# Gated linear attention and an ELU feed-forward in one kernel: blocks of 256 tokens taken in pairs from the fifth on

## The chip, the cores and the metric

The kernel runs on one core of a Trainium2 chip. The metric is the time of one execution on the device in microseconds (us), measured on runs without a profile; beside it there is one profiled execution with a trace of every engine. The engines are TensorE (PE, with its weight loads as PEld), VectorE (DVE), ScalarE (ACT), GpSimd (POOL) and SyncE (SP), which issues nearly all DMAs.

## The reference

```python
# q, k, v, alpha: (4, 8, 768, 48); w_in (384, 2048), w_out (2048, 384), all float32
for t in range(S):                       # per batch and head
    state = alpha[:, :, t, :, None] * state + einsum('bhd,bhe->bhde', k[:, :, t], v[:, :, t])
    y[:, :, t] = einsum('bhd,bhde->bhe', q[:, :, t], state)
x = y.transpose(0, 2, 1, 3).reshape(3072, 384)
h = x @ w_in
g = where(h > 0, h, exp(minimum(h, 0)) - 1)
out = g @ w_out
```

A recurrence over 768 tokens with a decay per token and channel, then two products with an ELU between them.

## The kernel before

The 3072 tokens are 24 windows of 128 (index i, six per batch) and 12 blocks of 256 (index b, two windows each). The state of a batch starts anew with every sixth window.

*Attention, per window.* L and LV load q, k, alpha and v. SC forms the running product P of the decays (a scan on VectorE), LN and EX its reciprocal R (ScalarE), KA, KB, KC and SQ scale k and q with them (POOL and DVE), T transposes k in 32x32 blocks on VectorE (eight instructions for a quarter g of the window's four). Then PE: U forms the two half-window updates of the state, S the scores of each half-window; both write a pair of PSUM banks named q. VectorE reads those banks: MK masks the scores (two parts), UA, UB and UC carry the state over the two halves and to the next window. Y multiplies state and masked scores into y, a bank of its own. XH (ScalarE) and XL (VectorE) split y into a high and a low part in f32r, written to the tile xt, which is the moving operand of the feed-forward; XD moves the channels of the last head pair to their rows by DMA.

*Feed-forward, per block b and j = 0 to 7.* A(b, j) multiplies 256 rows of w_in^T with x of the block: two slices f of 128 rows, each with 9 products (3 channel groups, and high x high, high x low, low x high), 256 columns each, into one bank h of 128 x 512. RA, RB (ScalarE), RC (VectorE) make the ELU, GH (ScalarE) and GL (VectorE, in some early blocks POOL) split it. O(b, j) multiplies with w_out into two banks per block, one for each 128 tokens: 12 products of 384 columns. Z copies the two banks out (ScalarE) and stores them. CA, CB, LC, V, VP check ranges of the weights, P and y for a slow path that is not taken here.

*Order.* Two tables written out by hand set the order: START names every step once with its indices up to O(3, 2), and STEADY is a table that function steady() unrolls for g = 4 to 13. One turn for one g is called a visit here: window indices stand relative to 2g, those of A to O relative to 8g (A.-3 is j = 5 of the block before, O.-5 is j = 3 of it), Z relative to g. Each engine executes its own steps nearly in the order of the tables; semaphores between engines and the reuse of buffers do the rest. All PSUM tiles share one pool of eight banks (psa, tag "pa"): a bank that q, y or h held goes to the next tile when its last reader is done. The x tile of a block is in a pool of two.

In STEADY of before a visit's Y is that of windows 2g and 2g + 1, and U and S are those of 2g + 2 and 2g + 3. The lines of the profile: U L368, S L323, Y L452 (L447 early), A L650, O L703, RA L658, RB L663, RC L669, GH L675, GL L689, MK L351, UA and UB L405 (UA on ScalarE L403 in windows 6, 12, 18), UC L434, SC L201, T L284, SQ L253, XH L506 and L507, XL L529 and L533, XD L540, Z L712, CA L601, CB L606. In the changed kernel most of them are three later up to L540, and nine or more later from A on.

Of the kernel before, what the change touches and what calls it, by code (L numbers as in the profile page):

```python
# [8 lines left out]
F32 = mybir.dt.float32  # L9
F32R = mybir.dt.float32r  # L10
# [70 lines left out]
MK.2.1 UC.2 XD.1 ZV.4 O.-4 XD.0 RC.-3 CB.-12 SC.4 RB.-2 A.-1 PC.3 GH.-3 RC.-2 A.0 LN.4 GL.-3 UA.3 EX.4 RA.-1
GH.-2 LC.-11 MK.3.0 L.6 MK.3.1 UB.3 CA.-11 A.1 RA.0 KA.4 L.5 RB.-1 GL.-2 RC.-1 A.2 RB.0 UC.3 CB.-11 RA.1 GH.-1
RC.0 O.-3 KB.4 RB.1 SC.5 KC.4 LC.-10 GL.-1 LN.5 GH.0 EX.5 RC.1 T.4.1 O.-2 A.3 VP.0 CA.-10 T.4.2 GL.0 GH.1 A.4
T.4.3 KA.5 O.0 RA.2 GL.1 RB.2 RA.3 CB.-10 LV.5 RC.2 PC.4 GH.2 KB.5 RB.3 GL.2 LC.-9 O.1 O.-1 KC.5 RA.4 O.2 SQ.4
T.5.2 CA.-9 RB.4 RC.3 CB.-9 RC.4 GH.3 T.5.1 GH.4 T.5.0 GL.3 T.4.0 T.5.3 LC.-8 SQ.5 Z.-1 GL.4
"""

@with_exitstack
def gla_elu_ffn(ctx: ExitStack, tc: tile.TileContext, qka, vv, vn, wgt, out):
    nc = tc.nc  # L90
# [348 lines left out]
    xt = {}  # L439
# [14 lines left out]
                         start=start, stop=True, skip_group_check=True)  # L454

    def xs(i):
        blk, half = divmod(i, 2)
        if blk not in xt:
            xt[blk] = xpool.tile([128, 2, NC, 2, W], F32R, name="xt", tag="xt")
        return xt[blk][:, half]  # L460


    @tok
    def YL(i):
        d = win[i]
        if i >= DIRECT:
            return
# [32 lines left out]
    @tok  # L500
    def XH(i):
        d = win[i]
        x, y = xs(i), d["y"]
        if i >= DIRECT:
            y3 = d["y3"] = work.tile([128, 2, W], F32R, name="y3", tag="y3")
            nc.scalar.activation(out=y3[:, 0], in_=y[:, 3], func=AF.Copy, accum_out=chk_y[:, 1, i:i + 1])  # L506
        nc.scalar.activation(out=x[:, :, 0], in_=y[:, 0:3], func=AF.Copy, accum_out=chk_y[:, 0, i:i + 1])  # L507

    def rest(out, upper):

        nc.tensor.matmul(out, lhsT=minus, rhs=upper, start=False, stop=True, skip_group_check=True)  # L511

    @tok
    def XP(i):
        d = win[i]
        rest(d["y"][:, 0:3], xs(i)[:, :, 0])
        if i >= DIRECT:
            rest(d["y"][:, 3], d["y3"][:, 0])

    @tok  # L520
    def XL(i):
        d = win[i]
        x, y = xs(i), d["y"]
        if i >= DIRECT:
            y3 = d["y3"]
            if i in XPE:
                nc.scalar.copy(out=y3[:, 1], in_=y[:, 3])
            else:
                nc.vector.tensor_tensor(out=y3[:, 1], in0=y[:, 3], in1=y3[:, 0].bitcast(F32), op=ALU.subtract)  # L529
        if i in XPE:  # L530
            nc.scalar.copy(out=x[:, :, 1], in_=y[:, 0:3])
        else:
            nc.vector.tensor_tensor(out=x[:, :, 1], in0=y[:, 0:3], in1=x[:, :, 0].bitcast(F32), op=ALU.subtract)  # L533
# [10 lines left out]
    wgts = [None] * (2 * NJ)  # L544
# [92 lines left out]
    ff, ops_ = {}, {}  # L637

    @tok
    def A(b, j):  # L640
        x = xt[b]
        h = psa.tile([128, 2, BLK], F32, name="h", tag="pa")
        ff[b, j] = dict(h=h)
        for f in range(2):
            k = 0
            t = wgts[2 * j]
            for c in range(NC):
                ws = slice(f * DM + c * 128, f * DM + c * 128 + 128)
                for wi, xi in ((0, 0), (0, 1), (1, 0)):
                    nc.tensor.matmul(h[:, f, :], lhsT=t[:, wi, ws], rhs=x[:, :, c, xi].rearrange("p a x -> p x a"),  # L650
                                     start=(f == 0 and k == 0), stop=(k == 8), skip_group_check=True)
                    k += 1

# [37 lines left out]
    @tok  # L691
    def O(b, j):
        d = ff.pop((b, j))
        gh, gl = d["gh"], d["gl"]
        if j == 0:
            ops_[b] = [psa.tile([128, 512], F32, name="o", tag="pa") for _ in range(2)]
        for m in range(2):
            o = ops_[b][m]
            ms = slice(m * 128, m * 128 + 128)
            for f in range(2):  # L700
                t = wgts[2 * j + 1]
                for k, (gt, wi) in enumerate(((gh, 0), (gh, 1), (gl, 0))):
                    nc.tensor.matmul(o[:, 0:DM], lhsT=gt[:, f, ms],  # L703
                                     rhs=t[:, wi, f * DM:f * DM + DM].rearrange("p (a x) -> p x a", a=2),
                                     start=(j == 0 and f == 0 and k == 0),
                                     stop=(j == NJ - 1 and f == 1 and k == 2))

    @tok
    def Z(b):
        for m in range(2):  # L710
            ot = gpool.tile([128, DM], F32, name="ot", tag="ot")
            nc.scalar.copy(out=ot, in_=ops_[b][m][:, 0:DM])  # L712

            q = nc.sync if b < NBLK - 1 else nc.scalar
            q.dma_start(out=out[b * BLK + m * 128:b * BLK + m * 128 + 128, :], in_=ot)
        del ops_[b], xt[b]
# [33 lines left out]
    start = [t.split(".") for t in START.split()]  # L750
# [220 lines left out]
```

## Time and profile before

| | us |
|---|---|
| median of 3 runs | 479.66 (479.53 to 479.87) |
| profiled execution | 478.73 |
| its span, first to last instruction | 476.8 |
| PE busy in it | 469.3 |
| VectorE busy | 380.0 |
| ScalarE busy | 299.2 |
| POOL busy | 124.0 |

Matmuls are pipelined, so the length of one (277 ns for one of 256 columns on the page) is not what it costs in a row of them; the chain of work that ended last, in order of time, gives start, length and count of each piece on the path, and a piece divided by its count gives that cost. An fp32 product of the attention stands there as two records. A row of a view by windows of time has each engine's busy time with its count of instructions, the granted clock, the DMA share and GB/s. Rows of groups and of the timeline name the line, engine, operation, tiles out<-in, shapes and count.

### The profile page before, as it was taken

The numbers are of one execution on the slowest core, as the hardware profiler recorded it, in microseconds if no ns is written. First come the engines' busy times: TensorE is split into PE (matmuls) and PEld (weight loads), VectorE is DVE, ScalarE is ACT, GpSimd is POOL, SyncE is SP. The second block draws the span as 40 slices with busy tenths as digits, with TensorE's granted clock in tenths as the row PEclk, the third lists the DMA queues.
The fourth block names the chain that finished last, engine by engine and source line by source line (L and its number), as shares of the span: only waits on it lengthen the run. The fifth ranks groups of instructions, "written<-read, shape, count | busy, mean of one in ns | idle before, by whom it ended". The sixth has DMA issues, their size and how long they took to land.

```text
span 476.8 us, 13298 instructions
## 1 busy us (share of the span) xinstructions
PE 469.3 (98%) x5438; PEld 450.3 (94%) x5438; DVE 380.0 (80%) x770; ACT 299.2 (63%) x696; POOL 124.0 (26%) x111
## 2 busy tenths in 40 slices
PE   8999999999999999999999999999999999999995
PEld 4889999999999999999999999999999999999995
DVE  6989999789889979869989989878988998344321
ACT  4586668764764668756766765757765666554432
POOL 3012332534564602502602602602602500000000
PEclk9999999999999999999999999999999999999999
DMA  8999330712326056235235335334333321210011
GB/s 307 414 414 409 118 84 16 229 55 78 110 101 200 1 151 204 69 112 206 61 115 180 90 113 176 95 114 172 101 104 113 100 69 52 66 43 10 2 36 38
DMA packets 20483, 61.14 MB, mean 128 GB/s; under 512 B 2880, under 2 KB 7872, under 8 KB 20416
## 3 DMA queue, kind: packets, MB, share of 16 engines
q1 hardware_dynamic: 20128, 59.83, 37.3%
q8 instruction: 45, 0.74, 0.7%
q10 hardware_dynamic: 288, 0.39, 0.2%
q14 instruction: 22, 0.18, 0.1%
HBM read 53.53 MB, written 4.72 MB: 122 GB/s over the span
## 4 chain that ended last, share of the span: by engine, by line
PE 98%; ACT 0%; DVE 0%; POOL 0%; issue 0%; POOLq 0%; DVEq 0%
PE h L650 42%; PE o L703 39%; PE y L452 4%; PE q L368 2%; PE y L447 2%; PE q L323 2%; PE wp L126 2%; PE sc L339 1%; PE wd L623 1%; PE tp L274 1%; PE y L492 1%; PE u L386 1%; PE yl L447 0%; PE wd L511 0%; POOL gl L689 0%
## 5 line engine op out<-in xcount | busy, mean ns | idle before, releaser
L650 PE MATMUL h<-xt,w 128*128 128x256 f32 x1728 | 204.8, 277 | 0.5 <-DVE r L669 0.2
L650 PEld LDWEIGHTS h<-xt,w 128*128 128x128 f32 x1728 | 198.5, 192 | 4.2 <-issue 1.6
L703 PE MATMUL o<-w,gh 128*128 128x384 f32 x768 | 188.2, 327 | 0.0
L703 PEld LDWEIGHTS o<-w,gh 128*128 128x128 f32 x768 | 132.8, 189 | 0.5
L703 PE MATMUL o<-w,gl 128*128 128x384 f32 x384 | 125.6, 327 | 0.0
L658 ACT ACTIVATE r<-h 128x512 f32<-128x512 f32 x96 | 56.8, 594 | 41.7 <-PE h L650 34.5
L675 ACT CAST gh<-h 128x512 fp32r<-128x512 f32 x79 | 45.9, 583 | 58.4 <-DVE h L669 35.3
L284 DVE STREAM_TRANSPOSE kn<-qka 32x128 f32<-32x128 f32 x256 | 77.4, 302 | 4.0
L689 DVE TENSOR_TENSOR gl<-h,gh 128x512 fp32r<-128x512 f32 x79 | 54.1, 688 | 28.4 <-ACT gh L675 27.3
L703 PEld LDWEIGHTS o<-w,gl 128*128 128x128 f32 x384 | 72.6, 189 | 0.6
L223 POOL TENSOR_TENSOR qka<-qka,R 128x512 f32<-128x512 f32 x18 | 23.1, 1283 | 155.9 <-DVE gl L689 109.4
L669 DVE SCALAR_TENSOR_TENSOR h<-r,h 128x512 f32<-128x512 f32 x79 | 53.0, 688 | 12.1 <-ACT r L663 11.4
L663 ACT ACTIVATE r<-r 128x512 f32<-128x512 f32 x96 | 59.5, 634 | 0.9
L351 DVE TENSOR_TENSOR st<-q,mask 64x256 f32<-64x256 f32 x72 | 30.4, 422 | 9.0 <-ACT vs L403 7.2
L253 POOL TENSOR_TENSOR st<-qka,P 64x512 f32<-64x512 f32 x30 | 36.0, 1199 | 1.6
L228 POOL TENSOR_TENSOR R<-P,R 128x512 f32<-128x512 f32 x20 | 24.4, 1221 | 33.9 <-DVE qka L223 32.5
L689 POOL TENSOR_TENSOR gl<-r,gh 128x512 fp32r<-128x512 f32 x17 | 24.1, 1425 | 25.4 <-ACT gh L675 16.9
L201 DVE TENSOR_TENSOR_SCAN P<-qka,first 128x516 f32<-128x516 f32 x24 | 29.5, 1229 | 1.3 <-DMA qka<-in_qka_dram 0.8
L210 ACT ACTIVATE R<-P 128x512 f32<-128x512 f32 x24 | 15.1, 631 | 17.8 <-DVE P L201 17.8
L601 ACT ACTIVATE ck<-ck 128x384 f32<-128x384 f32 x32 | 22.2, 694 | 5.6 <-DMA ck<-in_wgt_dram 5.6
L606 ACT ACTIVATE ck<-ck,lim 128x384 f32<-128x384 f32 x32 | 24.6, 768 | 0.1
L233 DVE SCALAR_TENSOR_TENSOR qka<-R,qka 128x512 f32<-128x512 f32 x24 | 19.9, 827 | 1.5 <-POOL R L228 1.3
(105 smaller groups left out, 448.4 us busy)
## 6 DMA issues: line engine op xcount, KB each, us to landing
qka<-in_qka_dram SPq DMA_DIRECT2D x22, 770.0 KB, 5.6
raw<-in_wgt_dram SPq DMA_DIRECT2D x16, 768.0 KB, 13.4
ck<-in_wgt_dram SPq DMA_DIRECT2D x32, 384.0 KB, 3.3
vs<-in_vv_dram SPq DMA_DIRECT2D x36, 192.0 KB, 3.3
out_dram<-ot SPq DMA_DIRECT2D x22, 192.0 KB, 2.0
vs<-in_vv_dram SPq DMA_DIRECT2D x6, 384.0 KB, 9.9
xt<-y SPq DMA_DIRECT2D x40, 48.0 KB, 2.2
qka<-in_qka_dram SPq DMA_DIRECT2D x2, 512.0 KB, 4.8
```

Source lines behind the costliest of these rows:

```text
L201: nc.vector.tensor_tensor_scan(out=P.rearrange("p n w -> p (n w)"), data0=t[:, 2 * NP * W:], data1=first.rearrange("p n w -> p (n w)"), in ...
L253: eng(SQV, i).tensor_tensor(out=st[r, a], in0=d["q"][r], in1=pw(i)[r], op=ALU.mult)
L284: nc.vector.transpose(out=kn[32 * t:32 * t + 32, :, 32 * g:32 * g + 32], in_=d["kt"][32 * g:32 * g + 32, :, 32 * t:32 * t + 32])
L351: nc.vector.tensor_tensor(out=d["st"][r, a, :, c * C:(c + 1) * C], in0=d["s4"][a][o], in1=mask[o].unsqueeze(1).broadcast_to([64, NP, C]), ...
L606: nc.scalar.activation(out=t, in_=t, func=AF.Relu, scale=-1.0, bias=lim, accum_out=chk_w[:, 1, f:f + 1])
L650: nc.tensor.matmul(h[:, f, :], lhsT=t[:, wi, ws], rhs=x[:, :, c, xi].rearrange("p a x -> p x a"), start=(f == 0 and k == 0), stop=(k == 8) ...
L658: nc.scalar.activation(out=r, in_=d["h"], func=AF.Relu, scale=-1.0)
L663: nc.scalar.activation(out=d["r"], in_=d["r"], func=AF.Exp, scale=-1.0)
L669: nc.vector.scalar_tensor_tensor(out=d["g"], in0=d["r"], scalar=-1.0, in1=d["h"], op0=ALU.add, op1=ALU.max)
L675: nc.scalar.copy(out=gh, in_=d["g"])
L689: q.tensor_tensor(out=gl, in0=d["g"], in1=d["gh"].bitcast(F32), op=ALU.subtract)
L703: nc.tensor.matmul(o[:, 0:DM], lhsT=gt[:, f, ms], rhs=t[:, wi, f * DM:f * DM + DM].rearrange("p (a x) -> p x a", a=2), start=(j == 0 and f ...
```

## The change

From block 4 on (PB = 4), blocks 2n and 2n + 1 are a pair. One x tile holds the four windows of a pair. A(b, j) then takes one slice of 128 rows of w_in^T (row r = 8 (b mod 2) + j of 16) and the 512 tokens of the pair: 9 products of 512 columns into the bank h, where there were 18 of 256. O(b, j) takes that slice into four banks that stay open over both blocks of the pair: 3 products in each of four banks, where there were 6 in each of two. Z works once per pair: four copies, two on ScalarE and two on VectorE, from four buffers. In STEADY the visit that has U and S of a window now has its Y too (Y.2 and Y.3), so y of a window comes a visit earlier, and Y of windows 8 and 9 stands at the end of START. The scratch for dynamic DMAs shrinks to 2048 bytes. Blocks 0 to 3 are computed as before.

```diff
+PB = 4
 ...
 GL.3.3 O.3.0 TB.11 CB.3 SQ.10 PC.10 O.3.1 TA.11 LC.4 O.3.2
+Y.8 XH.8 XL.8 XD.8 Y.9 XH.9 XL.9 XD.9
 ...
 STEADY = """
-A.-3 Y.1 XH.1 Y.0 XH.0 A.-2 XL.1 RA.-3 O.-5 RA.-2 XL.0 LV.4 U.2 CA.-12 V.0 RB.-3 S.2 UA.2 MK.2.0 U.3 UB.2 S.3
...
+U.2 S.2 L.5 A.-3 MK.2.0 UA.2 UB.2 MK.2.1 UC.2 V.0 PC.3 SC.4 CA.-12 CB.-12 O.-5 U.3 S.3 RA.-3 LN.4 L.6 LC.-11 UA.3
+Y.2 MK.3.1 EX.4 MK.3.0 XH.2 O.-4 RB.-3 Y.3 XH.3 XL.2 A.-2 RC.-3 UB.3 GH.-3 RA.-2 RB.-2 XD.2 CA.-11 XL.3 GL.-3 UC.3
...
     def xs(i):
-        blk, half = divmod(i, 2)
-        if blk not in xt:
-            xt[blk] = xpool.tile([128, 2, NC, 2, W], F32R, name="xt", tag="xt")
-        return xt[blk][:, half]
+        pr, k = divmod(i, 4)
+        if pr not in xt:
+            xt[pr] = xpool.tile([128, 4, NC, 2, W], F32R, name="xt", tag="xt")
+        return xt[pr][:, k]
 ...
     def A(b, j):
-        for f in range(2):
+        x = xt[b // 2]
+        for f in range(2 if b < PB else 1):
             k = 0
-            t = wgts[2 * j]
+            r = 2 * j + f if b < PB else b % 2 * NJ + j
+            t = wgts[r // 2 * 2]
             for c in range(NC):
-                ws = slice(f * DM + c * 128, f * DM + c * 128 + 128)
+                ws = slice(r % 2 * DM + c * 128, r % 2 * DM + c * 128 + 128)
                 for wi, xi in ((0, 0), (0, 1), (1, 0)):
-                    nc.tensor.matmul(h[:, f, :], lhsT=t[:, wi, ws], rhs=x[:, :, c, xi].rearrange("p a x -> p x a"),
+                    if b < PB:
+                        o, xv = h[:, f, :], x[:, b % 2 * 2:b % 2 * 2 + 2, :, xi].rearrange("p a c x -> p c x a")[:, c]
+                    else:
+                        o = h.rearrange("p q x -> p (q x)")
+                        xv = x[:, :, c, xi].rearrange("p (q a) x -> p q x a", a=2)
+                    nc.tensor.matmul(o, lhsT=t[:, wi, ws], rhs=xv,
                                      start=(f == 0 and k == 0), stop=(k == 8), skip_group_check=True)
 ...
     def O(b, j):
+        pair = b >= PB
+        key = b // 2 * 2 if pair else b
+        r0 = b % 2 * NJ + j if pair else 2 * j
+        nf = 1 if pair else 2
+        if r0 == 0:
+            ops_[key] = [psa.tile([128, 512], F32, name="o", tag="pa") for _ in range(4 if pair else 2)]
+        for m, o in enumerate(ops_[key]):
+            for f in range(nf):
 ...
     def Z(b):
+        if b >= PB and b % 2 == 0:
+            return
+        for m, o in enumerate(ops_.pop(b0)):
+            ot = gpool.tile([128, DM], F32, name="ot", tag="ot", bufs=4)
+            if m % 2 and b >= PB:
+                nc.vector.tensor_copy(out=ot, in_=o[:, 0:DM])
+            else:
+                nc.scalar.copy(out=ot, in_=o[:, 0:DM])
+            q = nc.scalar if b == NBLK - 1 and m % 2 == 0 else nc.sync
 ...
-    nc = bacc.Bacc("TRN2", target_bir_lowering=False, num_devices=1)
+    nc = bacc.Bacc("TRN2", target_bir_lowering=False, num_devices=1, dynamic_dma_scratch_size=2048)
```

How the tables move PE's instructions, in one visit (g = 8, windows 16 to 19). The names are those of the tiles, out<-in; w is a tile of weights, vs holds state and v, qka holds k and q of a window; the rest of an O is left out. Before:

```order
L650 MATMUL h<-xt,w_861 128x256 x18
L452 MATMUL y<-st,vs_119 64x64 x16
L452 MATMUL y<-st,vs_118 64x64 x16
L650 MATMUL h<-xt,w_1138 128x256 x18
L703 MATMUL o<-w_851,gh 128x384 x2
...
L368 MATMUL q<-vs_120,kn 48x48 x16
L323 MATMUL q<-st,qka_132 64x64 x16
L368 MATMUL q<-vs_121,kn 48x48 x16
L323 MATMUL q<-st,qka_133 64x64 x16
L703 MATMUL o<-w_1086,gh 128x384 x2
```

PE does both Y of the visit between two A, and U and S of two windows between two O. After, on the same engine in the same visit:

```order
L371 MATMUL q<-vs_120,kn 48x48 x16
L326 MATMUL q<-st,qka_132 64x64 x16
L659 MATMUL h<-xt,w_1137 128x512 x9
L716 MATMUL o<-w_1085,gh 128x384 x2
...
L371 MATMUL q<-vs_121,kn 48x48 x16
L326 MATMUL q<-st,qka_133 64x64 x16
L455 MATMUL y<-st,vs_120 64x64 x16
L716 MATMUL o<-w_1441,gh 128x384 x2
...
L455 MATMUL y<-st,vs_121 64x64 x16
L659 MATMUL h<-xt,w_1137 128x512 x18
```

The small products now stand in three places of a visit where they stood in two, and an A is nine products of 512 columns.

The second place is the step from START to the first visit (g = 4, windows 8 to 11). PE before, from the last O of START:

```order
L703 MATMUL o<-w_851,gl 128x384
L650 MATMUL h<-xt,w_861 128x256 x13
L452 MATMUL y<-st,vs_119 64x64 x16
L452 MATMUL y<-st,vs_118 64x64 x16
L650 MATMUL h<-xt,w_1138 128x256 x18
L703 MATMUL o<-w_851,gh 128x384 x2
...
L368 MATMUL q<-vs_120,kn 48x48 x16
L323 MATMUL q<-st,qka_133 64x64 x16
```

and after:

```order
L716 MATMUL o<-w_850,gl 128x384
L455 MATMUL y<-st,vs_118 64x64 x16
L455 MATMUL y<-st,vs_119 64x64 x16
L371 MATMUL q<-vs_120,kn 48x48 x16
L326 MATMUL q<-st,qka_133 64x64 x16
L659 MATMUL h<-xt,w_860 128x256 x18
L716 MATMUL o<-w_850,gh 128x384 x2
```

Y of windows 8 and 9 comes right behind the last O of START, and U and S of window 10 right behind it, where an A and an O stood between. VectorE's order there, after:

```order
L287 STREAM_TRANSPOSE kn<-qka_134 32x4x32 x8
L256 TENSOR_TENSOR st<-qka_133,P 64x512 x2
L532 TENSOR_TENSOR y_2436<-y,y_2436 128x128
L536 TENSOR_TENSOR xt<-y,xt 128x3x128
L354 TENSOR_TENSOR st<-q,mask 64x4x64 x2
L408 TENSOR_TENSOR vs_120<-vs_120,q 48x192 x2
L532 TENSOR_TENSOR y_2460<-y,y_2460 128x128
...
L437 TENSOR_TENSOR vs_121<-q,P 48x192 x2
L204 SCALAR_TENSOR_TENSOR P<-qka_132,first 128x516
```

The transposes of window 11 and SQ of window 10 (st<-qka) stand where they stood; XL of window 8, MK and UA of window 10, XL of window 9, UC and the next scan follow them, with the other steps of window 10 between.

More of the change, by code (lines that the diff above doesn't have):

```diff
@@ L75 @@
 GL.3.3 O.3.0 TB.11 CB.3 SQ.10 PC.10 O.3.1 TA.11 LC.4 O.3.2
+Y.8 XH.8 XL.8 XD.8 Y.9 XH.9 XL.9 XD.9
 """
 STEADY = """
-A.-3 Y.1 XH.1 Y.0 XH.0 A.-2 XL.1 RA.-3 O.-5 RA.-2 XL.0 LV.4 U.2 CA.-12 V.0 RB.-3 S.2 UA.2 MK.2.0 U.3 UB.2 S.3
[L81 to L85, printed above, removed]
+U.2 S.2 L.5 A.-3 MK.2.0 UA.2 UB.2 MK.2.1 UC.2 V.0 PC.3 SC.4 CA.-12 CB.-12 O.-5 U.3 S.3 RA.-3 LN.4 L.6 LC.-11 UA.3
+Y.2 MK.3.1 EX.4 MK.3.0 XH.2 O.-4 RB.-3 Y.3 XH.3 XL.2 A.-2 RC.-3 UB.3 GH.-3 RA.-2 RB.-2 XD.2 CA.-11 XL.3 GL.-3 UC.3
+KA.4 KB.4 SC.5 A.-1 LN.5 EX.5 O.-3 ZV.4 RA.-1 RB.-1 XD.3 KA.5 KB.5 LV.4 RC.-2 GH.-2 CB.-11 A.2 KC.4 T.4.0 T.4.3
+RC.-1 GL.-2 KC.5 A.0 LC.-10 RA.2 GH.-1 GL.-1 LC.-9 T.5.3 T.5.0 RA.0 RB.0 RC.0 T.5.2 CA.-10 CB.-10 RB.2 RC.2 GH.0
+GL.0 O.-2 O.-1 Z.-1 A.1 RA.1 RB.1 RC.1 GH.1 A.3 RA.3 CA.-9 RB.3 T.4.2 GL.1 SQ.5 RC.3 CB.-9 A.4 T.4.1 SQ.4 RA.4 GH.2
+GL.2 RB.4 RC.4 GH.3 GL.3 T.5.1 GH.4 O.0 O.1 O.2 GL.4 LC.-8 VP.0 PC.4 LV.5
 """
@@ L640, in A @@
     def A(b, j):
-        x = xt[b]
         h = psa.tile([128, 2, BLK], F32, name="h", tag="pa")
         ff[b, j] = dict(h=h)
-        for f in range(2):
+        x = xt[b // 2]
+        for f in range(2 if b < PB else 1):
             k = 0
-            t = wgts[2 * j]
+            r = 2 * j + f if b < PB else b % 2 * NJ + j
+            t = wgts[r // 2 * 2]
             for c in range(NC):
-                ws = slice(f * DM + c * 128, f * DM + c * 128 + 128)
+                ws = slice(r % 2 * DM + c * 128, r % 2 * DM + c * 128 + 128)
                 for wi, xi in ((0, 0), (0, 1), (1, 0)):
-                    nc.tensor.matmul(h[:, f, :], lhsT=t[:, wi, ws], rhs=x[:, :, c, xi].rearrange("p a x -> p x a"),
+                    if b < PB:
[4 more added lines that the diff above has]
+                    nc.tensor.matmul(o, lhsT=t[:, wi, ws], rhs=xv,
                                      start=(f == 0 and k == 0), stop=(k == 8), skip_group_check=True)
@@ L694, in O @@
         gh, gl = d["gh"], d["gl"]
[L695 to L701, printed above, removed]
+        pair = b >= PB
[4 more added lines that the diff above has]
+            ops_[key] = [psa.tile([128, 512], F32, name="o", tag="pa") for _ in range(4 if pair else 2)]
@@ L702, in O @@
+        for m, o in enumerate(ops_[key]):
+            for f in range(nf):
+                r = r0 + f
+                t = wgts[r // 2 * 2 + 1]
+                at = f * BLK + m * 128
                 for k, (gt, wi) in enumerate(((gh, 0), (gh, 1), (gl, 0))):
[L703 to L706, printed above, removed]
+                    nc.tensor.matmul(o[:, 0:DM], lhsT=gt.rearrange("p q x -> p (q x)")[:, at:at + 128],
+                                     rhs=t[:, wi, r % 2 * DM:r % 2 * DM + DM].rearrange("p (a x) -> p x a", a=2),
+                                     start=(r == 0 and k == 0), stop=(r == 2 * NJ - 1 and k == 2))
@@ L708, in Z @@
     @tok
     def Z(b):
[L710 to L716, printed above, removed]
+        if b >= PB and b % 2 == 0:
+            return
+        b0 = b // 2 * 2 if b >= PB else b
+        for m, o in enumerate(ops_.pop(b0)):
[5 more added lines that the diff above has]
+            q = nc.scalar if b == NBLK - 1 and m % 2 == 0 else nc.sync
+            q.dma_start(out=out[b0 * BLK + m * 128:b0 * BLK + m * 128 + 128, :], in_=ot)
```

## The prediction

> **What bounds the kernel now.** I read the page first, then the chain in order of time, then the rows of VectorE and ScalarE at two places. The page says that one engine carries the whole span, and that two lines of it, the products of w_in (h, L650) and those of w_out (o, L703), make four fifths:
>
> ```profile
> span 476.8 us, 13298 instructions
> PE 469.3 (98%) x5438; PEld 450.3 (94%) x5438; DVE 380.0 (80%) x770; ACT 299.2 (63%) x696; POOL 124.0 (26%) x111
> PE 98%; ACT 0%; DVE 0%; POOL 0%; issue 0%; POOLq 0%; DVEq 0%
> PE h L650 42%; PE o L703 39%; PE y L452 4%; PE q L368 2%; PE y L447 2%; PE q L323 2%; PE wp L126 2%; PE sc L339 1%; PE wd L623 1%; PE tp L274 1%; PE y L492 1%; PE u L386 1%; PE yl L447 0%; PE wd L511 0%; POOL gl L689 0%
> ```
>
> So the time is a sum of what PE executes and of what keeps it waiting. One visit (one turn of STEADY) lasts 36.46 us; in it DVE is busy 31 to 33 us, so a delay of DVE can reach PE:
>
> ```profile
> 207.45:243.91 36.46, 36.46 (x434) 35.52 (x433) 30.97 (x72) 25.32 (x62) 9.66 (x8) 1.00 0.39 126
> 243.91:280.40 36.49, 36.45 (x433) 35.44 (x433) 32.66 (x77) 24.37 (x60) 10.01 (x10) 1.00 0.40 126
> ```
>
> The columns are PE, PEld, DVE, ACT, POOL, then the granted clock, 1.00 here. The chain in order of time, one visit and then single rows from others (start, us, what):
>
> ```profile
> 205.44 2.02 PE y L452 x64
> 207.45 2.21 PE h L650 x18
> 209.66 1.95 PE o L703 x12
> 211.61 0.51 PE q L368 x32
> 212.12 0.48 PE q L323 x32
> 212.59 0.41 PE q L368 x29
> 213.52 2.15 PE o L703 x12
> 215.67 8.39 PE h L650 x72
> 227.97 4.02 PE h L650 x36
> ...
> 179.24 8.47 PE h L650 x72
> 397.98 8.28 PE h L650 x72
> 432.11 8.04 PE h L650 x72
> ```
>
> Read: 18 products of 256 columns (one A) take 2.01 us when nothing disturbs them (4.02 for 36, 8.04 for 72), which is 112 ns each; 12 products of 384 columns (one O) take 1.95, which is 162 ns. An A or O that follows small products of 64 rows or columns takes 0.20 more (2.21, 2.15). And in each of the seven visits from 179 to 398 us the four A behind the small products take 8.28 to 8.47 in place of 8.04: there they wait for VectorE to clear a bank.
>
> **The change, part by part.** The profiled execution took 478.73 us with a span of 476.8; the median of the runs is 479.66. I sum differences and put them on the median. Up to the third O of block 3 (about 163 us) all engines do the same in the same order, so what happens there costs nothing.
>
> *512 columns (64 of 96 A).* 18 products of 256 columns become 9 of 512. The only 512-column products of the profile are the warm-up's (bf16), once as ten, once as two:
>
> ```profile
> 7.18 2.32 PE L126 MATMUL wp<-first 128*128 128x512 bf16 x10
> 9.34 0.59 PE L126 MATMUL xf<-first 128*128 128x512 bf16 x2
> ```
>
> Eight more products cost 1.73 us, so 216 ns each. That is in line with O: 162 ns for 384 columns scales to 216 for 512. Nine make 1.94 us against 2.01: 0.07 saved per A, 64 times, **-4.5 us**. [...] The bounds: at 2 x 112 ns each it would save nothing (0); no row goes faster per column than 216 for 512, so the other end is what the rounding of 2.01 and 1.94 leaves, -5.1.
>
> *O in four banks.* Twelve products of 384 columns before and after, in threes per bank: 0. The copies out: 8 of 16 go from ACT to DVE, two per pair, at 0.55 us (a 128x384 read of PSUM, below). They stand behind the last O of a pair, and the next O of that bank comes three A (5.8 us) later, so 0; without that cover 1.1 us in each of 4 visits. At the end four copies stand where two stood; the bank that is done last is the fourth, and its copy (DVE, 0.55) follows the last product as ACT's did (0.83 for two): 0, with 0.3 as the other end. The larger x tile, four buffers for ot and the smaller scratch add no instruction and no DMA: 0.
>
> *The moved step's tail.* Y takes XH (ACT), XL (DVE) and XD (two DMAs per window from SP) with it. On SP they now stand behind L.6 and LC:
>
> ```profile
> qka<-in_qka_dram SPq DMA_DIRECT2D x22, 770.0 KB, 5.6
> xt<-y SPq DMA_DIRECT2D x40, 48.0 KB, 2.2
> ```
>
> L.6 can go when S is done, some 6 us ahead of XD, so XD waits for XL alone. By the times worked out below, XL of the second window ends 11 us after S and its pieces land 2.2 later, at 13.2; the first A that reads them (A.2) starts at 15.5: 0, covered by 2.3 us. On POOL (9.7 us busy per visit) nothing is passed but the memsets ZV, in two visits: 0.
>
> *Small products in more groups.* Per visit PE changes between small and full shape four times before (A to y, y to A, O to q, q to O). After, the groups are U S, then U S Y, then Y, each between full products: six changes, and one more between the shapes of S and y. That is 3 more in six visits, 4 more in the first and 2 fewer in the last: 20 changes. Leaving costs 0.20 (2.21 less 2.01). Entering is less plain: the first 32 U products take 0.51 against some 0.43 for the second 32. Between the two kinds of small products I have the early u, where 32 products change shape twice:
>
> ```profile
> 14.42 1.20 PE u L386 x32
> ```
>
> At the pace of y (2.02 for 64) they would take 1.01, so about 0.1 each is the least. I take 0.18 as the mean of 20 changes, nearer the 0.20 which is the best-measured row: **+3.6 us** (1.6 at 0.08, 4.0 at 0.20). [...]
>
> *The waits in the visits.* Seven times 8.28 to 8.47 against 8.04: 2.8 us in all. After the change the A that reuse these banks come later in the visit. What VectorE must do between S and the second y, from the rows of a visit before:
>
> ```profile
> 285.59 0.72 DVE L405 TENSOR_TENSOR vs<-vs,q 48x192 f32<-48x192 f32 x2 [1.90 <-PE q L323]
> 286.33 0.87 DVE L351 TENSOR_TENSOR st<-q,mask 64x256 f32<-64x256 f32 x2
> 287.24 0.76 DVE L405 TENSOR_TENSOR q<-vs,q 48x192 f32<-48x192 f32 x2
> 288.03 0.88 DVE L351 TENSOR_TENSOR st<-q,mask 64x256 f32<-64x256 f32 x2
> 288.83 0.73 DVE L434 TENSOR_TENSOR vs<-q,P 48x192 f32<-48x192 f32 x2
> 290.32 1.23 DVE L201 TENSOR_TENSOR_SCAN P<-qka,first 128x516 f32<-128x516 f32 x1
> 293.37 1.75 DVE L351 TENSOR_TENSOR st<-q,mask 64x256 f32<-64x256 f32 x4
> 282.29 0.28 DVE L529 TENSOR_TENSOR y<-y,y 128x128 fp32r<-128x128 f32 x1
> 282.49 0.55 DVE L533 TENSOR_TENSOR xt<-y,xt 128x384 fp32r<-128x384 f32 x1
> ```
>
> After: UA, MK, UB, MK, UC of the first window (0.72 + 0.87 + 0.76 + 0.88 + 0.73), the scan 1.23, UA 0.72, MK 1.75 of the second: 7.7 us until the second y may start. PE has between them an A (2.21 less 0.07), an O (1.95), U and S of one window (1.1), its partner's Y (1.1, half of 2.02 and a change of shape) and an O (2.15): 8.4 us. So 0.7 us are left. The A that takes the second y's bank needs XH from ACT and XL (0.28 + 0.55) and starts 2.1 us after that y; the same rows leave it 0.5. So the waits go: **-2.8 us** (the other end 0, if they only move).
>
> *The hand-over (first visit).* Y.8 and Y.9 now stand at the end of START with U.10 and S.10 right behind, before VectorE and ScalarE are ready; before, an A and an O stood between. Rows of before, whose order up to there stays:
>
> ```profile
> 155.32 7.80 PE o L703 x48
> 168.75 1.41 DVE L253 TENSOR_TENSOR st<-qka,P 64x512 f32<-64x512 f32 x2
> 170.19 2.51 DVE L284 STREAM_TRANSPOSE kn<-qka 32x128 f32<-32x128 f32 x8
> 170.51 0.83 ACT L712 COPY ot<-o 128x384 f32<-128x384 f32 x2
> 172.83 0.48 ACT L507 ACTIVATE xt<-y 128x384 fp32r<-128x384 f32 x1
> ```
>
> PE after: four O end at 163.1, two more at 167.0, Y.8 Y.9 at 169.0, U.10 at 169.7. S.10 needs st of L253, done 170.2: 0.5 waited. A(3,5) needs the bank that the first copy of ot clears, 170.9: 0.3. It ends 173.1, O 175.1, U.11 S.11 176.2. Y.10 needs MK.10: XL.8 cannot start before 173.3 (x of window 8 from ACT), then 0.7 for it, 0.9 MK, 0.7 UA, 0.7 XL.9, 0.8 UB, 0.8 MK: 177.9, so 1.7 waited. Y.11 needs UC, the scan, UA and MK behind that, 4.3 us: 182.2; PE is there at 181.2, so 1.0. PE takes its work in order: behind Y.10 wait O(3,4), Y.11 and A(3,6), and ACT waits for their y and h with nothing that is due earlier. Together **+3.5 us**; bounds 1.5 (if PE finds S.10 and Y.10 ready) and 4.5.
>
> Sum: -4.5 + 3.6 - 2.8 + 3.5 = -0.2 us, so 479.66 - 0.2 = **479.4 us**: four terms of the same size that cancel. About 0.2% (1 us) is what a measurement of this kernel can tell from no change.
>
> **The rivals.** *Faster.* Changes of shape cost 0.08 each when the group is already waited for or short (1.6 in place of 3.6) and the hand-over costs 2: -4.5 - 2.8 + 1.6 + 2 = -3.7, so 476. For it: the row of U (0.51 against 0.43). Against it: 2.21 and 2.15 in every visit.
>
> *Slower, by VectorE.* DVE does 33 us in visits that should shrink to 35.9, with up to 1.1 more in every second one; if it comes late before Y or before the A behind the second Y by 0.6 us in six visits, that is 3.6, so 483. Place: the second Y, which waits for MK, with a margin of 0.7; from a delay of 0.9 us per visit, and more than 1 us in all, it decides. For it: DVE reached PE in all seven visits before. Against it: the 7.7 against 8.4 above, and 1.90 of idle ahead of UA.
>
> *The wide product gives nothing*: 512 columns at 2 x 112 ns. Then -4.5 is 0 and the time 483.9. The bf16 rows and O speak against it, but no f32 product of 512 columns stands in the profile.
>
> **How the numbers follow.** Forecast, within 1 us of before: 0.37. Faster rival, with sums between: 0.35. VectorE late: 0.22. Wide product without gain: 0.06. So faster 0.35, same 0.37, slower 0.28. The range goes to the faster rival's 476 with 0.5 beyond, and to the slower one's 483 less 0.2: 475.5 to 482.8; the forecast's own is 478.2 to 480.7.
>
> **What would show it.** The page of after: 576 products of 128x512 in h; in the chain nine of them in 1.94 and an O in 1.95; three small groups per visit and about 35.9 us from visit to visit; no A stretched by a wait in the visits; PE idle or stretched at 169 to 182 us, ended by DVE st and ACT ot. Wrong would be: products of h over 220 ns, a wait for DVE st or xt in each visit, a hand-over without waits.

## The result: 0.8% slower, and the profile after

| | before | after |
|---|---|---|
| median of 5 runs, us | 479.66 (479.48 to 480.05) | 483.07 (482.62 to 484.79) |
| ratio | | 1.0081, 95% interval 1.0058 to 1.0104 |
| profiled execution, us | 478.73 | 484.79 |
| its span | 476.8 | 482.6 |

A second measurement of the changed kernel on another occasion gave 482.83 us and 1.0080 (1.0068 to 1.0093). The forecast was 479.4 us with a range of 475.5 to 482.8: the change was to save 0.2 us and cost 3.4 by the medians, 3.9 by the ratio. The profiled execution of the changed kernel, on which the next readings rest, is the slowest of its five.

The page of the changed kernel: span, busy time of the engines, and the chain by engine and by line.

```profile
span 482.6 us, 12096 instructions
PE 469.2 (97%) x4862; PEld 432.4 (90%) x4862; DVE 386.6 (80%) x778; ACT 304.4 (63%) x688; POOL 127.3 (26%) x111
PE 88%; DVE 4%; issue 2%; ACT 2%; DMA 1%; POOL 1%; SPq 0%; ACTq 0%; POOLq 0%; DVEq 0%
```

PE made 98% of the chain before; now 12% of it, 58 us, lies on other engines. PE is still busy for 97% of the span, so there are only some stretches in which it waited, and there the chain runs through those whom it waited for. They are not in the visits. This is one visit of the chain in order of time (start, us, what), from U of window 18 to U of window 20:

```profile
320.24 0.50 PE q L371 x32
320.74 0.48 PE q L326 x32
321.22 2.14 PE h L659 x9
323.36 1.95 PE o L716 x12
325.31 0.50 PE q L371 x32
325.82 0.48 PE q L326 x32
326.30 1.08 PE y L455 x32
327.38 2.15 PE o L716 x12
329.53 1.08 PE y L455 x32
330.61 4.08 PE h L659 x18
...
336.64 3.88 PE h L659 x18
...
344.43 5.83 PE h L659 x27
...
356.10 0.51 PE q L371 x32
```

Every piece is PE's, one behind the other: 35.86 us where 35.9 was forecast and 36.46 was before. Nine products of 512 columns take 1.94 (5.83 for 27), an A or O behind small products 0.20 more (2.14, 2.15, 4.08), and no A is stretched. So the visits do what the change says, and the loss is at their two ends.

*The hand-over.* VectorE and ScalarE at the step from START to the first visit, from the timeline (start, us, engine, line, what, and in brackets the idle time ahead and what ended it):

```profile
167.21 0.64 ACT L240 ACTIVATE R<-P 128x512 f32<-128x512 f32 x1 [2.60 <-DVE qka L236]
...
168.35 0.66 ACT L609 ACTIVATE ck<-ck,lim 128x384 f32<-128x384 f32 x1
...
169.74 1.41 DVE L256 TENSOR_TENSOR st<-qka,P 64x512 f32<-64x512 f32 x2
...
172.43 0.55 ACT L604 ACTIVATE ck<-ck 128x384 f32<-128x384 f32 x1 [3.33 <-DMA ck<-in_wgt_dram]
...
172.97 0.84 ACT L730 COPY ot<-o 128x384 f32<-128x384 f32 x2
...
175.31 0.49 ACT L510 ACTIVATE xt<-y 128x384 fp32r<-128x384 f32 x1
```

Three of these rows stand in the prediction for the kernel before: st at 168.75, the copies ot at 170.51, xt of window 8 at 172.83. VectorE's st came 0.99 later; that comes from the start of the execution (the first product of w_out, where both kernels still do the same, already came 0.98 later, at 58.40 against 57.42; last section). ScalarE's two came 2.46 and 2.48 later, so 1.5 us of it is new. The first row says why: PC of window 11 (L240) stood idle for 2.60 us until VectorE's KC (L236) was done, and GH, CB (L609), the load that CB lets go, CA (L604) and the copies stood behind it. In before, PC of window 11 was executed at 179 us. What PE waited for between 168 and 215 us:

```profile
PE h L659 <- ACT ot L730: 1.6, 1, 1.6
PE y L455 <- DVE st L354: 1.2, 1, 1.2
PE y L455 <- DVE xt L536: 0.6, 1, 0.6
PE q L326 <- DVE st L256: 0.4, 1, 0.4
```

(us in total, times, longest.) The first is the wait of A(3,5) for a bank, forecast at 0.3. And the rows by windows show one thing more (us, PE, PEld, DVE, ACT, POOL, granted clock, DMA share, GB/s):

```profile
178.00:180.00 2.00, 0.97 (x44) 0.72 (x38) 1.92 (x6) 1.76 (x5) 0.00 (x0) 1.00 0.73 284
180.00:182.00 2.00, 1.29 (x31) 1.22 (x32) 1.91 (x5) 0.00 (x0) 0.00 (x0) 1.00 0.22 57
182.00:184.00 2.00, 2.00 (x8) 2.00 (x8) 1.94 (x5) 1.36 (x4) 0.00 (x0) 0.54 0.67 200
184.00:186.00 2.00, 2.00 (x20) 1.56 (x20) 1.89 (x6) 1.25 (x6) 1.84 (x2) 0.61 0.93 374
```

Behind the waits the granted clock fell (0.54 over 182 to 184 us), and the one O there took 3.81 us in place of 1.95.

*The end.* One more wait of PE stands just ahead of the last product:

```profile
PE o L716 <- DVE gl L698: 0.3, 1, 0.3
```

The last three O took 6.51 us from the end of the last A (469.02 to 475.53), where before they took 5.87. O(11,6) waited for GL(11,6), which needs GH(11,6), and ScalarE did RA and RB of (11,7) first. So 0.7 us were lost there, in e1 and in the second profile of the changed kernel as well; no experiment took this wait away.

The last product ended at 471.96 of 476.80 us before and at 475.53 of 482.59 after: 4.8 us from there to the end, now 7.1. What happens in that time are the branches past the code for the slow path, which every engine takes when its own work is done, and the waits behind them. The rows of line 809, the branch, in the changed kernel (median length in ns, first and last start in us):

```profile
L809 SPq EVENT_SEMAPHORE  x8: 17/17/17, 480.5 to 481.0; - x8
...
L809 SPq COMPARE_BRANCH  x1: 45/45/45, 476.5 to 476.5; - x1
L809 ACTq COMPARE_BRANCH  x1: 54/54/54, 476.7 to 476.7; - x1
L809 DVEq COMPARE_BRANCH  x1: 72/72/72, 476.7 to 476.7; - x1
...
L809 ACTq EVENT_SEMAPHORE  x1: 17/17/17, 477.2 to 477.2; - x1
L809 DVEq EVENT_SEMAPHORE  x1: 21/21/21, 481.6 to 481.6; - x1
```

From its branch to its next instruction ScalarE needs 0.4 us, SP 3.9 and VectorE 4.8. Before, SP took this branch at 456.0 and VectorE at 469.8, where it cost nothing; now VectorE copies two of the last four banks and SP stores two of them, so both branch at 476.5 to 476.8, and are through 5.0 and 6.0 us behind the last product.

### The profile page after: what moved, and what is told of

Its sections match the earlier page's. It is cut to its first block, busy times and chain, and to the rows that moved or that the text cites. A ratio compares the mean times of both kernels' runs of the same rounds, so it can differ in the third digit from the quotient of the medians.

```text
span 482.6 us, 12096 instructions
## 1 busy us (share of the span) xinstructions
PE 469.2 (97%) x4862; PEld 432.4 (90%) x4862; DVE 386.6 (80%) x778; ACT 304.4 (63%) x688; POOL 127.3 (26%) x111
## 3 DMA queue, kind: packets, MB, share of 16 engines
HBM read 53.53 MB, written 4.72 MB: 121 GB/s over the span
## 4 chain that ended last, share of the span: by engine, by line
PE 88%; DVE 4%; issue 2%; ACT 2%; DMA 1%; POOL 1%; SPq 0%; ACTq 0%; POOLq 0%; DVEq 0%
PE h L659 37%; PE o L716 35%; PE y L455 4%; PE y L450 2%; PE q L371 2%; PE wp L129 2%; PE q L326 1%; PE sc L342 1%; PE wd L626 1%; DVE kn L287 1%; PE tp L277 1%; DMA ck<-in_wgt_dram 1%; DMA vs<-in_vv_dram 1%; PE y L495 1%; POOL gl L698 1%
## 5 line engine op out<-in xcount | busy, mean ns | idle before, releaser
L659 PE MATMUL h<-xt,w 128*128 128x256 f32 (+1 forms) x1152 | 199.0, 329 | 1.8 <-ACT ot L730 1.6
L659 PEld LDWEIGHTS h<-xt,w 128*128 128x128 f32 x1152 | 172.8, 190 | 17.6 <-ACT ot L730 1.7
L716 PEld LDWEIGHTS o<-w,gh 128*128 128x128 f32 x768 | 135.7, 190 | 2.4 <-ACT gh L684 0.2
L678 DVE SCALAR_TENSOR_TENSOR h<-r,h 128x512 f32<-128x512 f32 x79 | 54.3, 691 | 37.6 <-ACT r L672 36.9
L672 ACT ACTIVATE r<-r 128x512 f32<-128x512 f32 x96 | 60.8, 638 | 1.8
L256 POOL TENSOR_TENSOR st<-qka,P 64x512 f32<-64x512 f32 x30 | 38.9, 1297 | 1.4
L609 ACT ACTIVATE ck<-ck,lim 128x384 f32<-128x384 f32 x32 | 25.4, 795 | 0.5
L604 ACT ACTIVATE ck<-ck 128x384 f32<-128x384 f32 x32 | 22.3, 698 | 4.6 <-DMA ck<-in_wgt_dram 4.6
L455 PEld LDWEIGHTS y<-st,vs 128*64 128x64 f32 x576 | 18.3, 138 | 4.5 <-issue 2.0
```

The lines of the kernel that those rows point to most:

```text
L256: eng(SQV, i).tensor_tensor(out=st[r, a], in0=d["q"][r], in1=pw(i)[r], op=ALU.mult)
L455: nc.tensor.matmul(out[64 * a:64 * a + m], lhsT=lhs(i, c, a)[:, n * D:n * D + m], rhs=d["st"][:, a, n, c * C:(c + 1) * C], start=start, st ...
L659: nc.tensor.matmul(o, lhsT=t[:, wi, ws], rhs=xv, start=(f == 0 and k == 0), stop=(k == 8), skip_group_check=True)
L672: nc.scalar.activation(out=d["r"], in_=d["r"], func=AF.Exp, scale=-1.0)
L678: nc.vector.scalar_tensor_tensor(out=d["g"], in0=d["r"], scalar=-1.0, in1=d["h"], op0=ALU.add, op1=ALU.max)
L716: nc.tensor.matmul(o[:, 0:DM], lhsT=gt.rearrange("p q x -> p (q x)")[:, at:at + 128], rhs=t[:, wi, r % 2 * DM:r % 2 * DM + DM].rearrange(" ...
```

## Experiments

Times are medians with the ratio to the kernel before, measured on the same chip in the same rounds, where before had 479.1 to 479.2.

**ScalarE's order (e1).** One instruction moved, in the program of the first visit:

```diff
+    p.remove(("PC", 11))
+    p.insert(p.index(("RA", 3, 5)) + 1, ("PC", 11))
     return p
```

> The changed kernel with one instruction of ScalarE at another place: PC of window 11 (the check sum of P, L240) stands behind the first RA of the first visit, where before had it about; nothing else moves on any engine. Theory A (it waited there for VectorE's KC of window 11 and held up GH, CB, the load of LC, the two copies ot and XH of windows 8 and 9 behind it by 1.5 us): XH of window 8 starts some 1.5 us earlier, counted from the end of the row of O ahead of Y.8, and the time falls by 1.0 to 1.8 us, to about 481.6. Rival B (the hand-over is set by VectorE's transposes and masks, ScalarE is not on the path): the time stays within 0.4 us of the changed kernel. The chain of waits should in A no longer show ACT gh and ACT ck ahead of ot.

480.48 us, 1.0025 (1.0016 to 1.0033). In its trace PC no longer stands ahead of GH; the copies ot came 1.42 us behind st's start, where they came 3.23 behind it in the changed kernel, and PE's waits between 168 and 192 us are these:

```profile
PE y L455 <- DVE st L354: 1.2, 1, 1.2
PE y L455 <- issue: 0.6, 1, 0.6
PE q L326 <- DVE st L256: 0.4, 1, 0.4
PE y L455 <- DVE xt L536: 0.4, 1, 0.4
```

The wait for ot is gone, what is left is 2.6 us, and the granted clock stays at 1.00. So one check sum, off every chain itself, cost 0.56% or 2.7 us: more than theory A's 1.8, since the fall of the clock went with the wait (e10, below, has the two apart). Y of window 11 began at 182.00 us, where the prediction had worked out 182.2.

**The wide product (e3).** Each product of 512 columns as two of 256:

```diff
-                    nc.tensor.matmul(o, lhsT=t[:, wi, ws], rhs=xv, ...
+                    for p in range(1 if b < PB else 2):
+                        os, xp = (o, xv) if b < PB else (o[:, p * BLK:p * BLK + BLK], xv[:, p])
+                        nc.tensor.matmul(os, lhsT=t[:, wi, ws], rhs=xp, ...
```

> The changed kernel in which each product of 512 columns from block 4 on is written as two of 256 columns with the same weights; the order of all engines is unchanged. Theory A (the wide product itself saves 0.07 us per A, 64 times): the visits grow from 35.86 us to about 36.4 and the time by 4.5 us, to about 487.6. Rival B (the wide product saves nothing; the visits are short only because the waits for VectorE went): the time stays within 0.5 us and an A stays at 1.94 us. A part of it would show as a sum between 484 and 487.

488.25 us, 1.0182 (1.0167 to 1.0197): 4.8 us above the changed kernel by the two ratios. The same places of its chain:

```profile
321.29 2.21 PE h L661 x18
...
344.83 6.03 PE h L661 x54
```

2.21 and 6.03 where 2.14 and 5.83 stand above: 0.067 per A, 4.3 us in 64. Theory A holds: the visit grew to 36.4 us (U at 320.31 to U at 356.71). The 0.5 us between 4.3 and 4.8 stay open; in this profile the clock fell at another place of the hand-over (0.50 over 174 to 176 us).

**The end (e2, e8, e6).** e2: the last four copies and stores on ScalarE.

```diff
-            if m % 2 and b >= PB:
+            if m % 2 and PB <= b < NBLK - 1:
                 nc.vector.tensor_copy(out=ot, in_=o[:, 0:DM])
-            q = nc.scalar if b == NBLK - 1 and m % 2 == 0 else nc.sync
+            q = nc.scalar if b == NBLK - 1 else nc.sync
```

> The changed kernel with the last four copies of O all on ScalarE and their four stores on ScalarE's queue, as before did with its two. Nothing ahead of them moves. Theory A (in the changed kernel VectorE and SP have work up to the very end, and only then take the branch past the code that is not executed; 4.75 us pass from VectorE's branch to its next instruction, 3.9 us on SP, and this ends the span): the last store is now issued 1.2 us later, since one engine copies four banks, and lands about 2.2 us after its issue, but the span ends about 1.8 us after that, so 6.1 us after the last product in place of 7.0: 0.9 us faster, about 482.2. Rival B (the end is set by copies and stores, the branches are hidden): 1.2 us slower, about 484.3.

482.73 us, 1.0069 (1.0056 to 1.0082): between the theories, and in time not distinguishable from the changed kernel. The trace says more: VectorE branched at 471.5 and was through at 474.3, SP at 459.3, so no branch was left at the end. But the fourth store had been issued only 2.3 us after the last product, SP's wait for it ended at 5.1, and the span 6.7 us after that product. One cause had been exchanged for another.

e8 has e1's order and only the second part of that diff (VectorE copies, ScalarE's queue stores):

> The run with PC of window 11 moved, in which the two stores of SP at the end go to ScalarE's queue as well; the two copies on VectorE stay. SP's branch then comes early, VectorE's at the very end. Theory A (VectorE's branch past the code not executed, 4.4 to 4.9 us from branch to next instruction, ends the span): 6.3 to 6.6 us from the last product to the end, as with SP's stores. Rival B (SP's branch, 3.4 to 3.9 us, and its waits for the stores end it): 5.2 to 5.8 us.

One profiled execution, 480.7 us: 6.7 us from the last product to the end, nearest to A, but not for A's reason: VectorE was through at 4.25, and SP waited for the last store until 5.1. With SP's branch over at 5.0, VectorE's at 6.0 (changed kernel) and the last store at 5.1 (here and in e2), removing one shows the next.

e6 has e1's order, e2's edit, and O(11,6) and O(11,7) done bank by bank:

```diff
+        if (b, j) == (NBLK - 1, NJ - 2):
+            return
 ...
+        js = (j - 1, j) if (b, j) == (NBLK - 1, NJ - 1) else (j,)
+        ds = [ff.pop((b, x)) for x in js]
 ...
         for m, o in enumerate(ops_[key]):
+            for x, d in zip(js, ds):
```

> The run with PC of window 11 moved (480.5 us, 6.6 us from the last product to the end of the span), with the last four copies and stores on ScalarE, and O(11,6) and O(11,7) done bank by bank, six products each, so that the four banks close 0.97 us apart in place of 0.49. Same products, same banks. Theory A (the end is the later of two things: VectorE's branch, and the last store plus some 4.3 us; before had 4.8 from the last product): VectorE and SP branch early, ScalarE's copies keep pace with the banks, 4.8 to 5.0 us remain, and the time falls by 1.6 to 1.8 us to 478.7 to 478.9. Rival B (four stores at the end cost what they cost, whoever issues them): less than 0.8 us is won, 479.7 or more.

479.40 us, 1.0010 (0.9997 to 1.0022), 1.1 us below e1 by the medians and 0.7 by the ratios, so no clear case for either theory by the time alone. The profile has the gain at the end: 5.4 us are left from the last product, where e1 had 6.6. The branches now (the same rows as above):

```profile
L815 SPq COMPARE_BRANCH  x1: 45/45/45, 456.8 to 456.8; - x1
L815 DVEq COMPARE_BRANCH  x1: 72/72/72, 468.9 to 468.9; - x1
...
L815 DVEq EVENT_SEMAPHORE  x1: 21/21/21, 471.9 to 471.9; - x1
```

VectorE was through at 471.9, before the last product at 472.4. Theory A's direction holds, its size (1.6 to 1.8) only in part: the four stores still follow one another on one queue, and the issue of the third took 0.81 us where one alone takes 0.34 to 0.38. The wait for GL ahead of the last O also grew by 0.3 us, since each bank now needs both slices.

**The rest of the hand-over (e4, e5, e9).** e5 gives the first visit a table of its own, with PC moved as in e1 and PE's order changed in three places:

```diff
-U.2 S.2 L.5 A.-3 ... PC.3 SC.4 ... Y.2 ... O.-4 RB.-3 Y.3 XH.3 XL.2 A.-2
+A.-3 U.2 S.2 L.5 ... SC.4 ... RA.-3 PC.3 ... O.-4 Y.2 ... A.-2 Y.3 XH.3 XL.2
```

> The run with PC of window 11 moved (480.5 us), and in the first visit alone three places on PE changed: A(3,5) stands ahead of U and S of window 10, O(3,4) ahead of Y of window 10, A(3,6) ahead of Y of window 11. ScalarE's order is the same, on VectorE only the split of window 9 goes ahead of the mask of window 10. Theory A (what is left of the hand-over is PE waiting in order with full-size work ready behind it: 0.8 us in S.10, 0.4 in S.11, 1.5 in Y.10, 0.7 ahead of Y.11 in that run's trace, 3.4 in all): those waits go, the visit of windows 12 and 13 starts near 205.5, and the time falls by 2.5 to 3.4 us to 477.1 to 478. Rival B (VectorE's chain up to the second mask of window 11, then the two DMAs of x behind it, set the first A of block 4): the wait moves to that A, and less than 1.5 us are won, 479 or more.

479.29 us, 1.0004 (0.9995 to 1.0013): 1.2 us won by the medians, 1.0 by the ratios, which is Rival B's number. PE's waits there:

```profile
PE h L665 <- DMA xt<-y: 0.6, 1, 0.6
PE y L461 <- issue: 0.6, 1, 0.6
```

S.10 and Y.10 hardly wait any more, but the first A of block 4 now waits for the DMAs of x: part of the wait has moved.

e4 went further: all steps in one list, so that no engine takes anything from a later visit ahead, SQ of window 10 and Z of block 2 earlier, four full-size steps between the small groups.

```diff
-    with tc.manual_schedule():
-        for name, *at in start: ...
-    with tc.manual_schedule():
-        for name, *at in steady(): ...
+    with tc.manual_schedule():
+        for name, *at in start + [x for x in steady() if x not in start]: ...
```

> The changed kernel with another hand-over, all steps the same: from the last O of block 2 on, SQ of window 10 comes ahead of KC and the transposes of window 11, the copies Z of block 2 ahead of the check sums, U and S of window 10 ahead of the third O of block 3, and A(3,5), O(3,3), O(3,4), A(3,6) stand between S.10, Y.10, U.11 and Y.11; all steps are in one list, so that nothing of a later visit can go ahead of them. Theory A (7 us are lost at the hand-over: PE waits in order for VectorE and ScalarE, and the clock falls to 0.54 behind these waits): the visit of windows 12 and 13 starts 4 to 6 us earlier, the granted clock stays at 1.00 there, and the time falls to 477 to 479. Rival B (VectorE's sum of work between S.10 and the second mask of window 11 sets Y.11 whatever the order on PE): only the 1.5 us of ScalarE's order are won, about 481.5, and PE waits ahead of Y.11 or of the first A of block 4.

487.76 us, 1.0176 (1.0163 to 1.0189): the opposite. PE's waits between 190 and 217 us:

```profile
PE o L718 <- ACT gh L686: 3.6, 2, 2.9
PE o L718 <- DVE gl L700: 1.5, 1, 1.5
```

All O of block 3 were done by then; it is O(4,0) that waits. The chain there runs from POOL's KA of window 13 (197.56 us, against 187.90 in e7 below; KA of window 12 189.92 against 181.23) over KB, KC and the transposes to GL of block 4: VectorE takes its list in order, and with both windows late the transposes of window 13, waiting for POOL, stood ahead of the GL that PE needed; behind these waits the clock fell to 0.50 (208 to 212 us). e9 met the same from another side. It is e7 (next) with the scan of window 12 moved behind Y of window 11:

```diff
-UC.2 V.0 SC.4 ... RA.-3 PC.3 LN.4 L.6 ... EX.4 ... UC.3
+UC.2 V.0 ... RA.-3 PC.3 L.6 ... UC.3 SC.4 LN.4 EX.4
```

> The run with both changes (first visit reordered on PE, the end bank by bank; 478.4 us), in which the scan of window 12 and the Ln and Exp behind it stand after Y of window 11, its splits and UC, in the first visit alone. In that run's trace the scan (1.24 us) lies on VectorE ahead of UA and the mask of window 11, Y.11 waits 0.6 us for that mask, and the first A of block 4 waits 0.5 us for the DMAs of x. Theory A (these two waits hang on VectorE's chain): both go, and the time falls by 0.8 to 1.1 us to 477.3 to 477.6, some 0.35% below the kernel before. Rival B (the DMAs of x, or banks, set the first A of block 4): 478.2 or more.

483.19 us, 1.0095 (1.0080 to 1.0109). Y.11 waited no more, but:

```profile
PE o L726 <- DVE gl L704: 3.4, 1, 3.4
PE h L665 <- DMA xt<-y: 0.6, 1, 0.6
```

The 0.6 us that were to go with the scan stayed (B), and KC and eight transposes of window 12 came to stand, late, ahead of GL(3,6), which PE needed. Neither theory had looked behind the moved scan.

**Both repairs (e7)**: e5's table and e6's end.

> Both changes of this call together: first visit reordered on PE and PC of window 11 moved, and the end bank by bank on ScalarE alone. If each part is a place of its own on the chain, the gains add: 480.5 less 2.5 to 3.4 less 1.6 to 1.8, so 475.3 to 476.4 us, 0.6 to 0.8% below the kernel before. If one of the parts gave nothing, 477.5 to 478.5.

478.43 us (477.19 to 481.08), 0.9995 (0.9980 to 1.0009): the two gains roughly add (from the single runs 1.2 and 1.1 by the medians, 1.0 and 0.7 by the ratios; found 2.05 and 1.4), but both are smaller than their theories said, and against the kernel before this is no difference that can be measured. No version that beats before for certain was found.

**The changed kernel again (e10).**

> The changed kernel itself once more, for a second profile and for times on the same chip as the run beside it. If the hand-over with ScalarE's order as it is always leads to a fall of the clock: a row of O at half speed again between 178 and 188 us, the visit of windows 12 and 13 starts 56 to 57 us after the first O of block 3, against 53.3 with PC moved. If the fall comes only in some executions: 54.5 to 55.5 and a time near 482.

482.83 us. The clock fell again, at another place: 0.50 between 174 and 176 us, in A(3,5) itself. The visit of windows 12 and 13 started 55.0 us after the start of the row of six O that ends START (the mark from which the expectation's numbers count), against 56.4 in the first profile and 53.3 in e1. So neither branch of the expectation came as written: the clock fell again, but elsewhere, and in these two profiles the order on ScalarE cost the hand-over 1.7 and 3.1 us. In the second, Y of window 10 did not wait for its mask any more, so part of the fall was covered.

All eleven executions of the changed kernel have a mean granted clock of 0.992 or 0.993, the twelve of e1 0.996 to 0.999. A fall of 3.41 us to half takes 0.0035 off that mean. Two of e2's six, whose hand-over is the changed kernel's, have 0.998 and 0.999, so no fall, and took 482.43 and 482.10 us; the other four took 482.24 to 483.47, middle 483.1. From these few the clock's part of the 2.7 us is an estimate of some 0.9, and the rest is the wait.

## Why the prediction failed, step by step

| term | forecast, us | measured, us |
|---|---|---|
| 512 columns | -4.5 | -4.3 by the pieces, -4.8 by the ratio of e3 |
| shape changes | +3.6 | +2.6 to 3.0 |
| waits in the visits | -2.8 | -2.8: none is left |
| hand-over as worked out | +3.5 | +2.6 (e1's waits) |
| order up to the third O of block 3 | 0 | +2.7 (after to e1), with the clock |
| GL ahead of the last O | not in the sum | +0.7 |
| end | 0 to 0.3 | +1.7 (e1's 6.6 against 4.8) |
| sum | -0.2 | +3.2 to 3.6 |

The measured sum takes -4.3 for the first row, and for the end e1's profile, since the row of the order is the whole difference to e1; the end of the changed kernel itself is +2.2 and +2.4 in its two profiles. The medians differ by 3.4 and the ratio makes it 3.9.

- *Right:* the pace of the wide product, O in four banks, the visit of 35.9 us, VectorE's margin in the visits. The rival "VectorE late in six visits" gave 483, and the time is 483, but its mechanism did not occur: it has the number by chance.
- *Mis-sized: the shape changes.* The small products of a visit and the exits behind them take 4.72 us (0.50, 0.48, 0.50, 0.48, 1.08, 1.08 and three times 0.20); before they took 4.27 to 4.33. That is 0.13 to 0.15 for each of three changes, not 0.18: the exit is 0.20 as said, the entry only some 0.07 (1.08 against 1.01 for 32 products of y). So an entry cost about a third of an exit here.
- *Wrong: "up to the third O of block 3 all engines do the same in the same order, so what happens there costs nothing".* The diff adds only a line behind START, but the two tables are two lists, and only the order within each is fixed. PC of window 11 used to stand behind other ScalarE steps of the first visit; in the new table it is the first of them, and so it went ahead of the last steps of START and stood idle for 2.60 us. ScalarE's order before, at the end of START:

```
L675 CAST gh<-r 128x512
L675 CAST gh<-r 128x512
L606 ACTIVATE ck,chk_w<-ck,lim 128x384
L601 ACTIVATE ck,chk_w<-ck 128x384
L712 COPY ot<-o 128x384
```

and after:

```
L684 CAST gh<-r 128x512
L240 ACTIVATE R,chk_p<-P 128x512
L684 CAST gh<-r 128x512
L609 ACTIVATE ck,chk_w<-ck,lim 128x384
L604 ACTIVATE ck,chk_w<-ck 128x384
L730 COPY ot<-o 128x384
```

  The prediction compared PE and VectorE there, not ScalarE. With this one row put back (e1) the time fell by 2.7 us, and the waits of the hand-over came one by one within half a microsecond of what had been worked out: 0.4 for 0.5, 0 for 0.3, 1.6 for 1.7, 0.6 for 1.0.
- *Wrong: "its copy (DVE, 0.55) follows the last product as ACT's did".* It priced the copy and not what VectorE and SP do behind their last instruction. Both branches were in the trace of before, 2.8 us on VectorE and 3.1 on SP, hidden because both engines were done early. They are one of two causes of the longer end: with both out of the way, four stores on one queue still left 6.7 us (e2), and only e6, which also let the four banks close further apart, came to 5.4. What an engine does in the time between its branch and its next instruction (4.8 us on VectorE, 3.9 on SP, 0.4 on ScalarE) no run shows.

## What to carry to other kernels

Where two hand-written lists meet, compare every engine's order across the seam, the idle ones too: an instruction on no chain can stop an engine that works in order (here 2.60 us on ScalarE), and the waits it makes cost more when the clock falls behind them (here 2.7 us, some 0.9 of it put to the clock by the estimate above). Price the end of a kernel by which engines work last, not by the length of their last instruction. And before an instruction is moved later, follow what it releases over the other engines back to the list that it left: that is what e4 (7 us above e1) and e9 (5 above e7) lost.

## What the runs showed of the hardware

- *The clock fell to 0.50 behind waits that together made up about half of 3.41 us.* Each fall in the hand-over of the two profiles of the changed kernel and of e2 and e3 lasted 3.4 us (3.41 in the first profile), at 0.50. In the 3.41 us ahead of it PE was busy for 1.75 us in the first profile (idle for 0.55 and 1.18, with a little work between), 1.55 in e10, 1.68 in e2 and 1.73 in e3. In e1 the least that PE was busy in such a stretch of the hand-over was 1.88, and it kept 1.00. That share alone does not tell when the clock falls: in the first profile the waits of 0.4 and 1.6 us at 171 to 173 left PE busy for only 1.43 of the 3.41 us up to 173.47, and the clock stayed at 1.00 there. Taken in steps of 3.41 us back from the fall these waits lie in two stretches, the later of which has 1.86; whether that is why it stayed no run shows (the rows of windows, PE's busy time behind the length):

```profile
171.92:175.33 3.41, 1.86 (x16) 1.86 (x17) 1.70 (x6) 2.90 (x11) 0.00 (x0) 1.00 0.31 109
178.74:182.16 3.42, 1.75 (x34) 1.57 (x35) 3.26 (x8) 1.06 (x3) 0.00 (x0) 1.00 0.34 110
182.16:185.57 3.41, 3.41 (x12) 2.99 (x10) 3.28 (x9) 2.60 (x8) 1.41 (x2) 0.50 0.85 299
```

- *The branch at the end took VectorE 2.7 to 4.8 us.* From its end to the next instruction it was 2.8 us in before, 2.7 in e2 and 2.9 in e6, where VectorE branched ahead of the last product, and 4.8 in the changed kernel, 4.4 in e1 and 3.5 in e8, where it branched behind it; why the second is longer no run shows.
- *The start of an execution moved what follows by up to 1 us.* The warm-up products followed one another 0.43 us apart at first and 0.22 apart later. Their rows in the first 12 us of four runs (busy, mean ns), of before, the changed kernel, e1 and e10:

```profile
L126 PE MATMUL wp<-first 128*128 128x512 bf16 x25 | 7.4, 468 | 2.1 <-DVE first L120 2.1
L129 PE MATMUL wp<-first 128*128 128x512 bf16 x25 | 8.5, 522 | 2.1 <-DVE first L123 2.1
L129 PE MATMUL wp<-first 128*128 128x512 bf16 x25 | 7.0, 448 | 2.1 <-DVE first L123 2.1
L129 PE MATMUL wp<-first 128*128 128x512 bf16 x25 | 7.3, 463 | 2.1 <-DVE first L123 2.1
```

  They began at 2.1 us each time and changed to the faster pace at 5.9 us in before and at 8.1 in the changed kernel; for e1 the estimate is 5.0, from the end of its row and the two paces. The 0.99 us by which VectorE's st was late above is this, and no effect of the change: in e10, the same kernel, st came at 168.72, and before had it at 168.75. The row of six O that ends START began at 155.15 us in before and at 156.15 in the first profile of the changed kernel; single profiles are compared from a mark behind the start.
